# All tokens of k and v five to a partition on 116 partitions, the last one in a transfer of its own

## Chip, cores, metric

One core of one Trainium2 chip. The metric is device time in microseconds (us) of one execution. The profile is a hardware trace of one execution; its span is some 2 us shorter than the time that is measured for that run.

## The reference

Linear attention with the map elu + 1, followed by one feed-forward layer with GELU (tanh form), float32 in and out:

```python
# q, k, v: (8 batches, 8 heads, 576 tokens, 64)   w_in: (512, 2048)   w_out: (2048, 512)
phi = lambda x: np.where(x > 0, x, np.exp(x) - 1.0) + 1.0
q_p, k_p = phi(q), phi(k)
kv  = einsum('bhsd,bhse->bhde', k_p, v)
z   = sum(k_p, axis=2)
num = einsum('bhsd,bhde->bhse', q_p, kv)
den = einsum('bhsd,bhd->bhs', q_p, z)[..., None] + 1e-06
x   = (num / den).transpose(0, 2, 1, 3).reshape(4608, 512)
out = gelu(x @ w_in) @ w_out
```

For the argument one number counts: a batch has 576 tokens, which is 4.5 x 128.

## The kernel before

Of each batch, 512 tokens of q, k and v are loaded four to a partition on all 128 partitions. The other 64 (the "rest") of two batches share a tile of 128 partitions and come in small transfers. The main loads, the weights and the transposing transfers are all issued from SyncE, in program order, into one queue; 20 of the 24 transfers of rests come from GpSimd, and the stores from ScalarE.

```python
P = 128; C = 4; MAIN = P * C; REST = S - MAIN            # 512 and 64
pld = ctx.enter_context(tc.tile_pool(name="pld", bufs=6))  # loads and weights on their way in
psm = ctx.enter_context(tc.tile_pool(name="psm", bufs=2))  # transposed rests of q (qtr)

def load_main(src, b, name, eng, parts=1):
    t = pld.tile([P, H, C * D], FP32, name=name, tag="ld")
    hs = H // parts
    for i in range(parts):
        eng.dma_start(
            out=t[:, i * hs : (i + 1) * hs, :],
            in_=src[b, i * hs : (i + 1) * hs, 0:MAIN, :].rearrange(
                "h (p c) d -> p h (c d)", c=C))
    return t

def load_rest_half(src, t, m, s, eng):
    eng.dma_start(out=t[REST * s : REST * (s + 1)],
                  in_=src[2 * m + s, :, MAIN:S, :].rearrange("h p d -> p h d"))

def load_batch(b):
    for n, src in (("k", k), ("q", q), ("v", v)):
        ld[n, b] = load_main(src, b, n + "_x", nc.sync)

def kv_mm(b, i, kv_ps, at_i=None):                        # per pair of heads
    # ... cut: dst, kp, kr
    for c in range(C):
        nc.tensor.matmul(dst, lhsT=kp[:, c, P * i : P * (i + 1)],
                         rhs=vps[b % 2][:, 2 * i : 2 * i + 2, c, :], start=(c == 0), stop=False)
    nc.tensor.matmul(dst, lhsT=kr[:, 0, P * i : P * (i + 1)],   # the rests, in a matmul of their own
                     rhs=vrs[(b // 2) % 2][b % 2][:, 2 * i : 2 * i + 2, :], start=False, stop=True)

def qtr():                                                # q of a batch, by transposing transfers
    phis("q")
    qts[b] = pt.tile([P, C, NP, P], BF16, name="qt")
    for c in range(C):
        nc.sync.dma_start_transpose(out=qts[b][:, c],
                                    in_=phi["q", b][:, c].rearrange("p h d -> p (h d)"))
# ... cut: q @ kv (n_ps) waits for qt; x goes through transposes to h_ps (first GEMM), GELU, o_ps (second GEMM)

for b in range(4, B):
    at(2, b - 3, 2 if b == 4 else 0, lambda b=b: load_batch(b))   # the loads of b, ahead of qtr of b - 1
```

## Time and profile before

| | before |
|---|---|
| median of 4 runs (lowest to highest) | 296.93 us (295.47 to 297.31) |
| TensorE (PE) busy, granted clock | 97% of the span, 1.00 |
| transfers, whole queue when full | 406 GB/s |
| first n_ps matmul of batches 1, 2, 3, 4, 5, 6, 7 | 47.2, 77.6, 96.4, 121.4, 151.6, 181.8, 211.5 us |

The granted clock is the share of its full clock that TensorE was given. The page gives the busy share of every engine, then its course in 40 slices of the span (a digit is tenths), then the chain of work that ended last. Its lines are quoted in the prediction below. The starts of n_ps, read from the trace's list of matmuls, are the clock of this kernel: n_ps of a batch is the first matmul that needs the batch's transposed q. Before the change matmuls set the pace from 40 us on.

### The profile page before, as it was taken

To read this page: it belongs to the slowest core of one execution; us is meant where nothing else is said; L and a number is where in the kernel's file an instruction comes from. 1 tells how busy PE (TensorE), PEld (TensorE's weight loads), DVE (VectorE), ACT (ScalarE), POOL (GpSimd) and SP (SyncE) were. 2 spreads that over 40 slices of the span, in tenths; PEclk is the share of its full clock that TensorE was granted. 3 is DMA by queue.
4 is the path that set the end of the run, shared out by engine and by line. 5 is a ranking of instruction groups with operands and counts; after the bars stand their busy time and mean duration, and the time that the engine had idled before them with its cause. 6 is when DMAs were issued, how large, how long until landed. Compare 5 with 4: busy or idle time off the path is not lost.

```text
span 293.6 us, 4284 instructions
## 1 busy us (share of the span) xinstructions
PE 285.3 (97%) x1701; PEld 149.8 (51%) x1730; DVE 114.4 (39%) x189; ACT 159.2 (54%) x221; POOL 37.1 (13%) x56
## 2 busy tenths in 40 slices
PE   8999999999999999999999999999999999999995
PEld 6885446644565545544454445544554444444443
DVE  3660576245486684356125652543241000000002
ACT  4657963679955772567255935682560176017400
POOL 8057077400005200000000000000000000000000
PEclk9999999999999999999999999999999999999999
DMA  7999999994599969949913895304241110021032
GB/s 238 328 405 394 370 363 384 318 363 143 151 345 243 185 203 341 190 59 288 307 65 71 245 312 126 71 2 139 75 62 30 71 74 0 4 94 47 0 71 71
DMA packets 63731, 53.23 MB, mean 181 GB/s; under 512 B 31712, under 2 KB 56544, under 8 KB 63712
## 3 DMA queue, kind: packets, MB, share of 16 engines
q1 hardware_dynamic: 60288, 41.82, 50.7%
q10 hardware_dynamic: 2464, 8.52, 7.4%
q0 software_dynamic: 960, 2.62, 3.4%
q8 instruction: 13, 0.21, 0.3%
q14 instruction: 6, 0.05, 0.1%
HBM read 36.70 MB, written 9.44 MB: 157 GB/s over the span
## 4 chain that ended last, share of the span: by engine, by line
PE 84%; DMA 11%; DVE 2%; POOL 1%; issue 1%; SPq 0%; ACT 0%; DVEq 0%
PE o_ps L734 39%; PE h_ps L306 37%; DMA w_st<-in_moe_w_out_dram 8%; DMA q_x<-in_q_dram 3%; PE n_ps L258 3%; PE kv_ps L224 2%; PE o_ps L703 1%; POOL w_out_sb L153 1%; PE t_ps L281 1%; DVE kvbd L247 1%; PE kv_ps L231 1%; SPq L67 0%; ACT q_e L165 0%; PE t_ps L252 0%; DVE xt L388 0%
## 5 line engine op out<-in xcount | busy, mean ns | idle before, releaser
L734 PE MATMUL o_ps<-w_out_sb,g 128*128 128x512 bf16 x547 | 123.7, 379 | 1.3 <-POOL w_out_sb L153 0.4
L306 PE MATMUL h_ps<-xt,w_in_sb 128*128 128x512 bf16 (+2 forms) x566 | 118.9, 353 | 0.8
L691 ACT ACTIVATE g<-h_ps 128x512 bf16<-128x512 f32 x144 | 84.4, 598 | 49.9 <-PE h_ps L306 49.0
L734 PEld LDWEIGHTS <-g 128*128 128x128 bf16 x560 | 54.1, 98 | 63.5 <-issue 1.1
L306 PEld LDWEIGHTS <-w_in_sb 128*128 128x128 bf16 x644 | 58.2, 98 | 54.4 <-issue 0.5
L749 ACT COPY o_sb<-o_ps 128x512 f32<-128x512 f32 x18 | 10.5, 585 | 57.7 <-PE o_ps L734 53.1
L747 DVE COPY o_sb<-o_ps 128x512 f32<-128x512 f32 x17 | 11.7, 689 | 64.5 <-PE o_ps L734 57.2
L270 DVE TENSOR_TENSOR x<-n_ps,r 128x512 bf16<-128x512 f32 x36 | 24.9, 692 | 1.2
L247 DVE CAST kvbd<-kv_ps 64x260 bf16<-64x260 f32 (+1 forms) x16 | 6.5, 409 | 39.2 <-PE kv_ps L231 39.1
L165 ACT ACTIVATE q_e<-q_x 128x2048 bf16<-128x2048 f32 (+1 forms) x10 | 15.5, 1557 | 3.1 <-DMA q_x<-in_q_dram 3.1
L165 ACT ACTIVATE k_e<-k_x 128x2048 bf16<-128x2048 f32 (+1 forms) x9 | 15.5, 1719 | 2.8 <-DMA k_x<-in_k_dram 2.7
L268 DVE RECIPROCAL r<-n_ps 128x8 f32<-128x8 f32 x36 | 7.4, 206 | 24.0 <-PE n_ps L258 24.0
L182 DVE TENSOR_TENSOR k_p<-k_p,k_e 128x2048 bf16<-128x2048 bf16 (+1 forms) x9 | 10.7, 1193 | 13.5 <-ACT k_e L165 13.3
L333 PE MATMUL w_ps<-warm 128*128 128x252 bf16 x94 | 14.0, 315 | 1.1 <-DVE warm L124 1.1
L176 DVE TENSOR_SCALAR q_p<-q_x 128x2048 bf16<-128x2048 f32 (+1 forms) x10 | 10.7, 1068 | 8.8 <-DMA q_x<-in_q_dram 8.8
L306 PE MATMUL h_ps<-xt_rest,w_in_sb 128*128 128x512 bf16 x62 | 13.9, 379 | 0.1
L258 PEld LDWEIGHTS <-qt 128*128 128x128 bf16 x128 | 9.7, 98 | 7.9 <-issue 1.0
L208 DVE CAST vp<-v_x 128x2048 bf16<-128x2048 f32 (+1 forms) x9 | 9.4, 1045 | 9.9 <-DMA v_x<-in_v_dram 9.9
L258 PE MATMUL n_ps<-kvbd,qt 128*128 128x130 bf16 x128 | 12.7, 221 | 0.6 <-ACT kvbd L247 0.2
L224 PEld LDWEIGHTS <-k_p 128*128 128x128 bf16 x128 | 9.6, 96 | 6.1 <-DVE vp L208 0.7
L224 PE MATMUL kv_ps<-vp,k_p 128*128 128x130 bf16 x128 | 11.9, 220 | 0.4 <-DVE vp L208 0.4
L333 PEld LDWEIGHTS <-warm 128*128 128x128 bf16 x94 | 10.4, 114 | 3.2 <-DVE warm L124 1.1
(52 smaller groups left out, 141.3 us busy)
## 6 DMA issues: line engine op xcount, KB each, us to landing
out_dram<-o_sb ACTq DMA_DIRECT2D x16, 512.0 KB, 4.9
k_x<-in_k_dram SPq DMA_DIRECT2D x7, 1024.0 KB, 5.9
v_x<-in_v_dram SPq DMA_DIRECT2D x7, 1024.0 KB, 12.4
q_x<-in_q_dram SPq DMA_DIRECT2D x6, 1024.0 KB, 9.0
w_st<-in_moe_w_in_dram SPq DMA_DIRECT2D x4, 1024.0 KB, 10.1
w_st<-in_moe_w_out_dram SPq DMA_DIRECT2D x4, 1024.0 KB, 11.3
q_x<-in_q_dram SPq DMA_DIRECT2D x4, 512.0 KB, 9.9
k_x<-in_k_dram SPq DMA_DIRECT2D x2, 512.0 KB, 4.1
```

The source lines that it names most:

```text
L165: nc.scalar.activation(e[:, :, hs, :].rearrange("p c h d -> p h c d"), by_chunk(x[:, hs]), AF.Exp)
L176: nc.vector.tensor_scalar(xp[:, :, hs, :].rearrange("p c h d -> p h c d"), by_chunk(x[:, hs]), 1.0, 1.0, op0=ALU.add, op1=ALU.max,)
L182: nc.vector.tensor_tensor(xp[:, :, hs, :], xp[:, :, hs, :], e[:, :, hs, :], op=ALU.min)
L224: nc.tensor.matmul(dst, lhsT=kp[:, c, P * i : P * (i + 1)], rhs=vps[b % 2][:, 2 * i : 2 * i + 2, c, :], start=(c == 0), stop=False,)
L258: nc.tensor.matmul(n_ps[rows, i // 2, 2 * E * (i % 2) : 2 * E * (i % 2) + 2 * E], lhsT=qt_c[:, i, rows], rhs=kvbd[:, i, :], skip_group_che ...
L270: nc.vector.tensor_tensor(x, n_v[:, :, :, 0:D], r[:, :, :, None].to_broadcast([P, 2, 4, D]), op=ALU.mult,)
L306: nc.tensor.matmul(h_ps[:, tok], lhsT=w_in_sb[:, c, P * m : P * (m + 1)], rhs=xt[:, c, tok], start=(c == 0), stop=(c == KM - 1), skip_grou ...
L333: nc.tensor.matmul(w_ps[:, 0:252], lhsT=warm[:, 0:P], rhs=warm)
L691: nc.scalar.activation(gs[j][:, i, :], ps, AF.Gelu_apprx_tanh)
L734: nc.tensor.matmul(o_pss[t], lhsT=g[:, m, P * t : P * (t + 1)], rhs=w_out_sb[:, m, :], start=(m == 0), stop=(m == MM - 1),)
L747: nc.vector.tensor_copy(dst, o_ps)
L749: nc.scalar.copy(dst, o_ps)
```

## The change

The intent is to have no rest of k and v any more: 575 tokens lie five to a partition on 115 partitions, the last token's five-group (tokens 571 to 575, four of them loaded twice) on partition 115 by a transfer of its own, and only partition 115's fifth token is used. That takes away the small rest loads, their maps and casts and GpSimd's clearing of their tiles. To make room, the pools psm and px lose a buffer each. Cut to the core:

```diff
+    CK = 5
+    PK = S // CK          # 115
+    RK = PK + 1           # 116
-    psm = ... bufs=2      px = ... bufs=5
+    psm = ... bufs=1      px = ... bufs=4
+    def load_kv(src, b, name, parts=1, eng=nc.sync):
+        t = staged(name, LD).rearrange("p (h x) -> p h x", h=H)
+        eng.dma_start(
+            out=t[PK:RK],
+            in_=src[b, :, S - CK : S, :].rearrange("h (p c) d -> p h (c d)", c=CK),
+        )
+        hs = H // parts
+        for i in range(parts):
+            s = slice(i * hs, (i + 1) * hs)
+            nc.sync.dma_start(
+                out=t[0:PK, s],
+                in_=src[b, s, 0 : PK * CK, :].rearrange("h (p c) d -> p h (c d)", c=CK),
+            )
+        return t[0:RK]
     def load_batch(b):
-        for n, src in (("k", k), ("q", q), ("v", v)):
-            ld[n, b] = load_main(src, b, n + "_x", nc.sync)
+        ld["k", b] = load_kv(k, b, "k_x")
+        ld["q", b] = load_q(b, "q_x", nc.sync)      # q as before
+        ld["v", b] = load_kv(v, b, "v_x")
     # kv_mm:
-        for c in range(C):
+        for c in range(CK):
+            r = slice(0, RK if c == CK - 1 else PK)
             nc.tensor.matmul(
                 dst,
-                lhsT=kp[:, c, P * i : P * (i + 1)],
-                rhs=vps[b % 2][:, 2 * i : 2 * i + 2, c, :],
+                lhsT=kp[r, c, P * i : P * (i + 1)],
+                rhs=vps[b % 2][r, 2 * i : 2 * i + 2, c, :],
-        nc.tensor.matmul(dst, lhsT=kr[...], rhs=vrs[...], ...)
# ... cut: all loads, maps, casts and memsets of kr and vr go; q's rests stay
```

## The prediction

> **What bounds the kernel now.** I read the page first. Its second part says where the time is and where it is not: the tensor engine is busy 97% of the span at the full granted clock, and the transfers are near full only in the first third.
>
> ```profile
> span 293.6 us, 4284 instructions
> PE 285.3 (97%) x1701; PEld 149.8 (51%) x1730; DVE 114.4 (39%) x189; ACT 159.2 (54%) x221; POOL 37.1 (13%) x56
> ...
> PEclk9999999999999999999999999999999999999999
> DMA  7999999994599969949913895304241110021032
> ...
> PE 84%; DMA 11%; DVE 2%; POOL 1%; issue 1%; SPq 0%; ACT 0%; DVEq 0%
> ```
>
> The last line is the chain that ended last: 84% matmuls, 11% transfers, next to nothing else. The 11% lie wholly at the start. The chain in order of time, for the first 45 us, shows it:
>
> ```profile
> 2.34 8.66 DMA q_x<-in_q_dram
> ...
> 14.28 13.33 DMA w_st<-in_moe_w_out_dram
> 27.66 8.97 DMA w_st<-in_moe_w_out_dram
> 36.68 3.02 POOL w_out_sb L153 x2
> 39.75 1.89 PE o_ps L734 x8
> ```
>
> So up to about 40 us the kernel runs at the pace of the transfer queue, and from there at the pace of matmuls. Next, how fast the queue is when it is full. A window from 15 to 25 us, and the queue's own row:
>
> ```profile
> 15.00:25.00 10.00, 9.35 (x130) 7.73 (x129) 4.89 (x13) 5.48 (x10) 6.07 (x6) 1.00 1.05 406
> ...
> q1 hardware_dynamic: 60288, 41.82, 50.7%
> ```
>
> All 16 engines are busy (share 1.05) and move 406 GB/s, 25.4 GB/s each. The queue q1 of SyncE holds all loads of k, q, v and the weights and also all the transposing transfers. Last, the transposes, once behind loads and once on a quiet queue (the tile qt, windows 87 to 93 and 199 to 206 us):
>
> ```profile
> L465 SPq DMA_TRANSPOSE qt<-q_p x4: 1257/1262/1637, 87.4 to 91.7; - x4
> ...
> DMA to landing us min/median/max: 3.5/4.8/5.5
> ```
>
> ```profile
> L465 SPq DMA_TRANSPOSE qt<-q_p x4: 1191/1257/1264, 200.0 to 203.9; - x4
> ...
> DMA to landing us min/median/max: 2.3/2.4/2.4
> ```
>
> The reader is to see that a transpose takes 2.3 us alone and up to 5.5 us behind a load. The completion records agree: v of batch 4 lands at 92.36 us and the transpose issued at 87.35 lands at 92.89. It waited in the queue for the loads ahead of it.
>
> **What the Trainium skill says.** (1) "DMA: Bandwidth & Descriptors", section "Why a DMA increments its semaphore by 16 and not by 1": a transfer is cut along the slowest dimension of both access patterns, over the largest number k of engines, at most 16, that divides both sizes; on the SyncE and ScalarE queues these are the lowest-numbered k; 100 partitions give 10, 127 give 1. In the kernel before every plain transfer has 128 or 64 rows outermost, so k is 16 and no run yet shows another k. (2) Same page, "Queues, rings and completion order": on each engine one queue's work is consumed in the order of issue. The transposes above agree. (3) "TensorE: Matmul & The Clock Gate", Part 1: an idle window of some 3.4 us halves the clock. Not seen before (1.00 in every window), and possible after.
>
> **The change, part by part.** *Removed:* 16 rest loads of k and v (128 KB each, 4 from SyncE and 12 from GpSimd), the GpSimd memsets of vr and kr_p in the first 8 us, five kr maps and eight vr casts. *Added:* a fifth token on each partition, and a one-partition transfer per load. Vector and scalar work nets out: with 2560 columns for 2048 the k exp goes from 1.91 to about 2.33 us, and two batches add 0.84, against one 0.61 us kr exp removed; on VectorE the three k and v operations gain some 0.85 us a batch, 1.7 for two, against 0.42 + 0.42 + 2 x 0.42 = 1.7 removed. Matmuls stay five for a head pair, 160 in all. None of this is on the chain, so without the transfers I would call it 297 us.
>
> *The transfers are what moves.* The main load has 115 partitions outermost on both sides, 115 = 5 x 23, so by the skill's rule it runs on engines 0 to 4 alone. Cost of a load: with a full queue, k and q of batch 2 land 2.72 and 2.81 us after what is ahead of them; an engine's share is 64 rows of 1024 B, so 42 ns a row. Weight loads land 2.56 us apart for 32 rows of 2048 B, 80 ns a row. The line through both gives 51.6 ns for a row of 1280 B. Each of five engines gets 23 partitions x 8 heads = 184 rows: **9.5 us a load in place of 2.7** (an estimate; 124 GB/s). There are 16 such loads, and engines 0 to 4 still do their sixteenth of everything else.
>
> *The first stage.* The first half of k lands at 4.48 us with 1.35 us of transfer, so 3.1 us are fixed. Before, to the end of v of batch 3: 3.1 + 12 x 2.7 (k, q, v) + 8 x 2.56 (weights) + 2.8 (four rests on SyncE) + 2.6 (two stores) + 5.9 (rests of GpSimd) = 67.3 us; it landed at 71.7, so 4.4 us are unexplained and I keep them. After: 3.1 + 8 x 9.5 + 4 x 2.7 + 20.5 + 2.6 + 2.0 + 4.4 = 119.4 us. On the way v of batch 0 lands at about 25 us (before 14.8) and v of batch 1 at about 65 to 68 (before 43.0): the matmuls start 10 us late, and are 22 to 24 us late in the second half of batch 0. Then the transposes of batch 2's q stand in the same queue behind v of batch 3, and its first n_ps matmul, at 77.6 us before, has to wait for about 120: **+42 us**.
>
> *The later stages.* The program issues the loads of batch b+1 ahead of the q transposes of batch b, and every such transpose now waits for two loads of 9.5, one of 2.7 and two stores of 1.3 us: 24.3 in all. Batch 3: 119.4 + 2.9 (four transposes of 0.72) + 24.3 + 0.5 = 147 us for 96.4 before, +51. From there it is a loop: n_ps begins; the four x transposes and the next k load follow after 8.0 us (batch 3) or 10.7 us (batches 4, 5), as before; then 2.4 us to start, 24.3 of transfers, 0.5 to the first transpose. Batch 4: 147.1 + 8.0 + 27.2 = 182.3 for 121.4, +61. Batch 5: 182.3 + 10.7 + 27.2 = 220.2 for 151.6, +69. Batch 6: 258.1 for 181.8, +76. The period is 37.9 us where matmuls alone need 30.2. Batch 7 has no load behind it; from 181.8 us on the kernel before needs 111.8 us, mostly matmuls. Sum: 258.1 + 111.8 = 369.9 span, and the medians lie 3.5 us over the span: 373. As stores and loads share the queue better than a plain sum, and five engines may each run a little faster than sixteen do together (7% would make a load 8.9 us, and 16 x 0.6 = 10 us less), I take **368 us**.
>
> **Rivals.** (a) *The load still uses 16 engines* (the software reorders or splits it): then the small rest transfers go and nothing on the chain changes but the queue of the first 40 us, which gets four rests (2.8 us) shorter: 293 to 298 us. For it: the rule was not seen at work in this trace. Against: the partition dimension can't be split into 16 and is always outermost. (b) *Five engines, but the later loads hide:* in 175 to 235 us the DMA row reads 1 to 5 tenths, which suggests room. Then only the first stage stays, +24 to +42 us: 321 to 339. Against: the transposes stand behind the loads in one queue, and a mean over 16 engines hides five full ones. (c) *Worse:* ScalarE issues the stores and may stand behind a transfer whose completion it waits for; before, it waited 4.6 us once for a v load.
>
> ```profile
> ACT o_sb L749 <- DMA v_x<-in_v_dram: 4.6, 1, 4.6
> ```
>
> If that happens with loads of 9.5 us, GELU stands too, and the tensor engine at half clock after each idle stretch adds 1 to 2 us a batch: 385 to 400.
>
> **Range and chances.** The load time is the great lever: 1 us more or less on it is 16 us. With 8.3 to 10.5 us, and the overlaps of (b) and (c), 338 to 398. Faster by over 2% would need rival (a) and more: 0.02. Within 2%: (a), 0.05. Slower: 0.93.
>
> **What would show it.** Right: k_x and v_x take 9 us or more to land even first in the queue (before, 3.7 at the least); packets of 1280 B in q1; the window around 200 us has the DMA row at three or four tenths for long while PE idles; waits of PE or VectorE for qt; n_ps of batch 2 at about 120 us; a period near 38 us from batch 4 to 6; the last 110 us unchanged. Wrong: a whole-queue rate over 300 GB/s while k or v is loaded, or PE still at 97%; then (a) holds. PE full from 130 us on would mean (b). Long ScalarE waits for a load ahead of a store would mean (c).

## The result

The changed kernel takes **421.22 us** (420.45 to 422.62, 4 runs) against 296.93 us (295.47 to 297.31, 4 runs): 1.42 times as long, with a 95% interval of 1.414 to 1.428. A ratio here is the mean time of one kernel's runs over that of the other's of the same rounds, so not quite the ratio of the medians that are quoted. Executions over 1.5% slower than the fastest of the same kernel are left out of the means. The output is correct. Direction and mechanism are as predicted; the size is not: 421 lies above the range of 338 to 398.

The page of the changed kernel, with the lines that answer to those of before, and the row of GB/s:

```profile
span 419.2 us, 4288 instructions
PE 308.7 (74%) x1730; PEld 159.5 (38%) x1730; DVE 111.5 (27%) x171; ACT 160.5 (38%) x216; POOL 24.9 (6%) x35
...
PEclk9767986899965797599769985899679999999999
DMA  4499394593369579456833469237841431101113
GB/s 121 140 240 374 127 204 144 143 230 141 119 166 123 125 238 136 109 117 215 127 72 63 142 203 145 50 103 234 118 87 35 129 49 65 52 0 50 52 25 75
...
PE 48%; DMA 39%; SPq 9%; DVE 2%; issue 1%; ACT 0%; DVEq 0%
```

In many slices the DMA row reads 3 to 5 where it read 9 before: a third of the engines, not a quiet queue. The chain is 39% transfers and 9% SyncE's sequencer (SPq), for 11% and 0% before. The clock is below 1 in most slices of the first three quarters, 0.865 in the mean.

Two windows of the changed kernel. The columns are the window, its length, busy times by engine, then clock, mean busy share of the 16 DMA engines, GB/s:

```profile
22.00:30.00 8.00, 1.91 (x18) 1.24 (x16) 0.92 (x2) 1.28 (x2) 0.00 (x0) 0.71 1.08 239
105.00:115.00 10.00, 6.68 (x31) 2.84 (x29) 2.74 (x2) 5.41 (x7) 0.00 (x0) 1.00 0.34 119
```

In the second a k or v load is alone: 5 of 16 engines busy, 119 GB/s. The first is the surprise: all engines are busy as in the window of before that moved 406 GB/s, and they move 239.

Where the tensor engine stands for it, from the waits of the changed kernel (us in total, times, longest):

```profile
PE n_ps L248 <- DMA qt<-q_p: 67.9, 5, 16.5
...
DVE vp L210 <- DMA v_x<-in_v_dram: 42.6, 4, 21.1
```

And the chain of waits in order of time (start, duration, what), its longest transfers alone:

```profile
30.25 51.71 DMA w_st<-in_moe_w_out_dram x3
...
122.18 16.60 DMA qt<-q_p
...
151.87 19.86 DMA qt<-q_p
...
205.93 6.03 DMA qt<-q_p
...
244.18 16.95 DMA qt<-q_p
...
286.40 18.28 DMA qt<-q_p
```

Up to 82 us the weights come late because the k and v loads stand ahead of them; then, once a batch, a transposed q ends a wait. Their ends are the starts of n_ps, side by side with the prediction:

| n_ps of | before | predicted | measured | excess over predicted |
|---|---|---|---|---|
| batch 2 | 77.6 | 120 | 138.8 | 19 |
| batch 3 | 96.4 | 147.1 | 171.8 | 25 |
| batch 4 | 121.4 | 182.3 | 212.0 | 30 |
| batch 5 | 151.6 | 220.2 | 261.2 | 41 |
| batch 6 | 181.8 | 258.1 | 304.7 | 47 |
| end of the span | 293.6 | 369.9 | 419.2 | 49 |

### The profile page after: what moved, and what is told of

It reads as the page before. It is cut to its first block, busy times and chain, and to the rows that moved or that the text cites. A ratio compares the mean times of both kernels' runs of the same rounds, so it can differ in the third digit from the quotient of the medians.

```text
span 419.2 us, 4288 instructions
## 1 busy us (share of the span) xinstructions
PE 308.7 (74%) x1730; PEld 159.5 (38%) x1730; DVE 111.5 (27%) x171; ACT 160.5 (38%) x216; POOL 24.9 (6%) x35
## 4 chain that ended last, share of the span: by engine, by line
PE 48%; DMA 39%; SPq 9%; DVE 2%; issue 1%; ACT 0%; DVEq 0%
PE o_ps L702 24%; PE h_ps L296 20%; DMA qt<-q_p 19%; DMA w_st<-in_moe_w_out_dram 12%; DMA v_x<-in_v_dram 9%; SPq L87 4%; PE n_ps L248 2%; SPq L77 2%; SPq L501 2%; SPq L94 1%; PE kv_ps L221 1%; PE o_ps L671 1%; DVE kvbd L237 0%; DVE vp L210 0%; DVE k_p L187 0%
## 5 line engine op out<-in xcount | busy, mean ns | idle before, releaser
L702 PE MATMUL o_ps<-w_out_sb,g 128*128 128x512 bf16 x560 | 130.5, 391 | 11.7 <-POOL w_out_sb L161 11.7
L296 PE MATMUL h_ps<-xt,w_in_sb 128*128 128x512 bf16 (+2 forms) x580 | 127.8, 370 | 0.2
L659 ACT ACTIVATE g<-h_ps 128x512 bf16<-128x512 f32 x144 | 84.4, 598 | 112.3 <-PE h_ps L296 111.5
L248 PE MATMUL n_ps<-kvbd,qt 128*128 128x130 bf16 x128 | 15.9, 260 | 67.9 <-DMA qt<-q_p 67.9
L248 PEld LDWEIGHTS <-qt 128*128 128x128 bf16 x128 | 12.0, 118 | 78.5 <-DMA qt<-q_p 70.5
L717 ACT COPY o_sb<-o_ps 128x512 f32<-128x512 f32 x18 | 10.6, 586 | 68.9 <-PE o_ps L702 68.9
L221 PE MATMUL kv_ps<-vp,k_p 115*128 115x130 bf16 (+1 forms) x160 | 15.9, 247 | 18.8 <-DVE vp L210 13.6
L173 ACT ACTIVATE k_e<-k_x 116x2560 bf16<-116x2560 f32 (+1 forms) x9 | 18.9, 2100 | 21.4 <-DMA k_x<-in_k_dram 21.3
L221 PEld LDWEIGHTS <-k_p 115*128 115x128 bf16 (+1 forms) x160 | 13.1, 110 | 25.7 <-issue 9.1
L210 DVE CAST vp<-v_x 116x2560 bf16<-116x2560 f32 (+1 forms) x9 | 11.4, 1269 | 42.6 <-DMA v_x<-in_v_dram 42.6
L187 DVE TENSOR_SCALAR k_p<-k_x 116x2560 bf16<-116x2560 f32 (+1 forms) x9 | 12.1, 1339 | 20.3 <-DMA k_x<-in_k_dram 20.3
L193 DVE TENSOR_TENSOR k_p<-k_p,k_e 116x2560 bf16<-116x2560 bf16 (+1 forms) x9 | 12.1, 1344 | 11.2 <-ACT k_e L173 11.0
L173 ACT ACT_TABLE_LOAD x7 | 9.0, 1283 | 14.5 <-DMA k_x<-in_k_dram 14.4
```

Source lines behind the costliest of these rows:

```text
L173: nc.scalar.activation(e[:, :, hs, :].rearrange("p c h d -> p h c d"), by_chunk(x[:, hs]), AF.Exp)
L187: nc.vector.tensor_scalar(xp[:, :, hs, :].rearrange("p c h d -> p h c d"), by_chunk(x[:, hs]), 1.0, 1.0, op0=ALU.add, op1=ALU.max,)
L193: nc.vector.tensor_tensor(xp[:, :, hs, :], xp[:, :, hs, :], e[:, :, hs, :], op=ALU.min)
L221: nc.tensor.matmul(dst, lhsT=kp[r, c, P * i : P * (i + 1)], rhs=vps[b % 2][r, 2 * i : 2 * i + 2, c, :], start=(c == 0), stop=(c == CK - 1),)
L248: nc.tensor.matmul(n_ps[rows, i // 2, 2 * E * (i % 2) : 2 * E * (i % 2) + 2 * E], lhsT=qt_c[:, i, rows], rhs=kvbd[:, i, :], skip_group_che ...
L296: nc.tensor.matmul(h_ps[:, tok], lhsT=w_in_sb[:, c, P * m : P * (m + 1)], rhs=xt[:, c, tok], start=(c == 0), stop=(c == KM - 1), skip_grou ...
```

## Experiments

Sixteen kernels ran. The kernel before took 295.65 to 296.59 us (medians) on the same chips. Engine counts are read from the trace as the 4-byte completion writes of a transfer: each engine that takes part writes one.

### 1. How many engines does a transfer use? (m_rate; wrong output on purpose)

```diff
+    for i, n in enumerate((128, 112, 96, 120, 100, 115, 116, 127, 1)):
+        nc.sync.dma_start(out=t[0:n], in_=k[i % B, :, 0 : 4 * n, :].rearrange("h (p c) d -> p h (c d)", c=4))
+    for i, n in enumerate((115, 112, 3, 1)):      # rows of five tokens
+        nc.sync.dma_start(out=t5[0:n], in_=v[i, :, 0 : 5 * n, :].rearrange("h (p c) d -> p h (c d)", c=5))
```

> Wrong result on purpose: it only loads, one transfer after another into one tile, so each waits until the one ahead has landed. Rows of 1024 B, 8 heads, n partitions outermost, SyncE's queue. Theory (the number of partitions sets the number of engines, the largest divisor up to 16): with 2.4 us fixed and 42 ns a row of an engine, issue to landing is 128: 5.1 us, 112: 4.8, 96: 4.4, 120 (15 engines): 5.1, 100 (10): 5.8, 115 (5): 10.1, 116 (4): 12.1, 127 (1): 45. The completion writes (packets of 4 B) number 16 for 128 and 5 for 115. Rival (all sixteen engines always, the slowness is elsewhere): all between 4 and 6 us. Then the changed kernel's own shapes with rows of 1280 B: 115: 11.9 us or 5, 112: 5.3, 3 partitions: 2.8, 1 partition: 2.5.

Completion writes: 128, 112 and 96 partitions 16; 120 partitions 15; 100: 10; 115: **5**; 116: 4; 127: 1; 3: 3. That is the rule of the Trainium skill, "DMA: Bandwidth & Descriptors", section "Why a DMA increments its semaphore by 16 and not by 1", in every case tried. 127 partitions on one engine took 45 us at 23 GB/s. The one-partition transfer has 8 writes: with one partition the next dimension, 8 heads, counts. The rates of the other shapes are not to be trusted: stores and loads of the same kernel ran beside them, a fault of its design. In the changed kernel itself the completion writes add up to exactly 18 main loads x 5 and 16 one-partition transfers x 8 (14 in SyncE's queue, 2 in ScalarE's), with 16 for every other transfer.

### 2. The engine count alone, in both kernels (a_112, b_115, b_112)

a_112 is the changed kernel with its main load cut into 112 + 3 partitions (16 engines and 3). b_115 and b_112 are the kernel before, with k and v cut into 115 + 13 and 112 + 16.

```diff
 # a_112, in load_kv of the changed kernel
+        eng.dma_start(out=t[112:PK], in_=src[b, :, 112 * CK : PK * CK, :]...)
-                out=t[0:PK, s], in_=src[b, s, 0 : PK * CK, :]...
+                out=t[0:112, s], in_=src[b, s, 0 : 112 * CK, :]...
 # b_115 (b_112: 112), in load_main of the kernel before
+            for p0, p1 in ((0, P),) if name == "q_x" else ((115, P), (0, 115)):
+                eng.dma_start(out=t[p0:p1, ...], in_=src[b, ..., C * p0 : C * p1, :]...)
```

> The changed kernel with each main load of k and v cut into 112 partitions (16 engines) and 3 partitions; everything else as changed, with one transfer more for each load. Theory (five engines are the cause of nearly all of it): granted clock back to 1.00, no wait of the tensor engine for qt, 295 to 305 us. Rival 1 (the extra small transfers stall the issue of the large ones): still 340 us or more, as there are now more of them. Rival 2 (smaller buffers psm and px): over 310 us with waits for qtr and xt.

> The kernel before with each main load of k and v cut into 115 and 13 partitions, rows of 1024 B as before; no other part of the change is in it. Theory: a load takes 8 us on five engines in place of 2.7, and all the waits of the changed kernel come with it, in size 8/10: 370 to 405 us. Rival (wide rows, one-partition transfers or smaller buffers are needed for the loss): under 310 us.

> The control for b_115: the same kernel before with each main load cut into 112 and 16 partitions, both of which 16 divides, so the same number of transfers as b_115 and as the changed kernel. Theory: same as before within 1% (294 to 300 us). Rival (an additional transfer for each load is itself the cost): over 310 us.

| kernel | time | ratio to before |
|---|---|---|
| a_112, 3 rounds | 325.81 us (323.79 to 332.69) | 1.096 (1.091 to 1.102) |
| b_115, one look | 387.36 us | |
| b_112, 3 rounds | 311.32 us (308.27 to 314.21) | 1.049 (1.042 to 1.057) |

b_115 has all the rests, both buffers and the arithmetic of the kernel before, and still loses 92 us, with the same wait (from its waits):

```profile
PE n_ps L259 <- DMA qt<-q_p: 42.3, 5, 11.4
```

So the partition count of the load is enough to make most of the loss (92 of 124 us). Going from 5 engines to 16 gives the changed kernel 95 of its 124 us back. But both 112 kernels are slower than expected: b_112 should have been within 1% of before and is 5% off. Sixteen engines are not the whole of it. (The profiled run of a_112 was its slowest, 332.7 us; the ratio does not use it.)

### 3. Rate by shape (m_ports; wrong output on purpose)

```diff
+    for lo, hi in ((0, 128), (0, 112), (0, 64), (64, 128), (0, 96), (0, 115), (0, 120)):
+        for i, t in enumerate(ts):                # six loads in a row, rows of 1024 B, nothing beside them
+            nc.sync.dma_start(out=t[lo:hi], in_=src[i, :, 0 : 4 * (hi - lo), :]...)
```

> Wrong result on purpose: loads alone, six in a row of each shape (rows of 1024 B, n partitions), nothing else on the queues. The cut of the changed kernel's load into 112 partitions used sixteen engines and still moved only some 215 GB/s. Theory (the partitions that engines write at the same time must lie at different ports of the on-chip memory, and 128 whole partitions are the arrangement that fits): 128: 390 GB/s, 112: 210 to 250, partitions 0 to 63: about 210, 64 to 127: about 210, 96: 200 to 260, 120 (15 engines): 200 to 260, 115: 118. Rival (the rate follows from the number of engines alone): 112, 96 and both 64: 390, 120: 365, 115: 118. Last, 128 and 115 in turn: by the theory a row of the 128 load takes longer than its 46 ns.

Windows in the stretches with 128, 112, 64 and 115 partitions (columns as above; GpSimd's busy time is the only engine's):

```profile
5.00:15.00 10.00, 0.00 (x0) 1.00 1.10 352
22.00:40.00 18.00, 0.00 (x0) 1.00 1.12 260
50.00:60.00 10.00, 0.00 (x0) 1.00 1.13 206
...
105.00:130.00 25.00, 0.00 (x0) 1.00 0.34 121
```

| partitions | engines | ns of a 1024-B row (median) | GB/s |
|---|---|---|---|
| 128 | 16 | 49 | 350 |
| 112 | 16 | 68 | 260 |
| 96 | 16 | 76 | 235 |
| 120 | 15 | 86 | 205 |
| 64, lower or upper half | 16 | 89 | 204 |
| 115 | 5 | 46 | 121 to 124 |

With 128, 112 and 64 partitions the engines are equally busy, and a row takes 49 to 89 ns. The Trainium skill, "SBUF — State Buffer", section "Door 1: The DMA port swizzle (why `[64,N]` ≈ `[32,N]`)", says that the rate depends on how many of 16 ports the partitions reach and that 64 partitions in one half reach 8; the run agrees (204 against 350). By the port table there partitions 0 to 111, and 0 to 95, reach all 16, so the count of ports alone does not give the 260 and 235 measured. "DMA: Bandwidth & Descriptors", section "The descriptor swizzle", says that in a transfer of 128 partitions each engine writes one port of its own. That other shapes lack this order would explain 112, 96 and 120; the trace has no port in its records, so this stays an inference. What is shown is the rate. (The last part of m_ports, 128 and 115 in turn, had stores beside it and is not read here.)

The rate alone does not close the sums of part 2. As an estimate, a load of 112 x 8 rows of 1024 B at 260 GB/s takes 3.5 us for 2.7 before, 16 x 0.8 = 13 us of b_112's 16, and one of 1280-B rows 4.4 us, some 27 of a_112's 30. But in the trace of b_112 n_ps of batch 2 is 12.7 us late after eight of the sixteen loads, 1.6 a load and not 0.8, and the other eight add 2 us. Its weight rows take 98 ns in the mean of the first 90 us for 86 before, so the loads beside slow down too. What the additional transfers cost, and in a_112 the single buffer of part 5, these runs do not separate.

### 4. Ten engines (a_110)

The diff is that of a_112 with 110 for 112: 110 + 5 partitions, ten engines and five.

> As a_112, but cut into 110 and 5 partitions: 110 gives ten engines of 11 partitions, so one step between the five of the changed kernel (421 us) and the sixteen of a_112 (326 us), with the same number of transfers. Theory (the number of engines sets it): a load takes 88 rows of 60 to 75 ns, 5.3 to 6.6 us; 335 to 365 us. Rival (a transfer is either spread well or not at all): at either end, under 330 or over 400 us.

371.17 us, somewhat above what was expected, and between 421 (five engines) and 326 (sixteen), as a dose would have it.

### 5. The rivals inside the program: order, tails, a single buffer (a_order, a_tailpool, a_rest)

```diff
 # a_order: loads of batches 4 to 7 behind the q transposes of the batch before
-        at(2, b - 3, 2 if b == 4 else 0, lambda b=b: load_batch(b))
+        at(2, b - 3, 15 if b == 4 else 6, lambda b=b: load_batch(b))
 # a_tailpool: the one-partition transfers of batches 4 to 7 from GpSimd
-        ld["k", b] = load_kv(k, b, "k_x")
+        ld["k", b] = load_kv(k, b, "k_x", eng=nc.gpsimd if b > 3 else nc.sync)     # v alike
 # a_rest: the transpose of the third rest of q at another place
-        plan_rest(m, (2, 2 * m - 2, 9), (1, 2 * m, 14))
+        plan_rest(m, (1, 3, 15) if m == 2 else (2, 4, 9), (1, 2 * m, 14))
```

> The changed kernel with the loads of a later batch issued after the q transposes of the batch ahead, not before them (batches 4 to 7); the same transfers. Theory (from batch 3 on the loss is that the transposes stand behind five-engine loads in one queue): the waits of n_ps for qt in batches 3 to 6 go, the wait at batch 2 stays (n_ps of batch 2 at about 139 us), 350 to 370 us. Rival (five engines are simply full, whatever the order): over 400 us, with the waits at k_x and v_x.

> The changed kernel with the one-partition transfers of batches 4 to 7 issued from GpSimd, off SyncE's queue. SyncE stood 4 to 6 us in each of these at 144, 188, 239 and 280 us. Theory (SyncE stands there only because the queue ahead is full; the small transfer is not a cost): within 1% of the changed kernel, 417 to 425 us. Rival (each stand delays the main load behind it): 395 to 412 us.

> The changed kernel with the transpose of the third q rest moved behind the first use of the second one, so that it does not wait for the single qtr buffer at 212 to 223 us at the head of SyncE's queue. Theory (that wait held back the x transposes and the loads of batch 6 by some 8 us): 409 to 415 us, and the loads of batch 6 issued 10 us after n_ps of batch 4, not 19. Rival (the loads of batch 6 were early enough anyway): 418 to 423 us.

a_order **417.73**, a_tailpool 420.42, a_rest 417.16 us (changed kernel 421.22).

a_order was my theory, and it fell as far as it was tried. If the loss were that transposes stand behind loads in one queue, turning them round should have given 50 us or more. It gave 4. The waits of a_order show where it went:

```profile
DVE vp L210 <- DMA v_x<-in_v_dram: 51.7, 5, 20.7
...
PE n_ps L248 <- DMA qtr<-qr_p: 33.4, 2, 19.7
```

The wait for qt turned into waits for v, k and the rest transposes (qtr). n_ps of batch 3 did begin 10.6 us earlier (161.1 for 171.8 us), but then TensorE stood 19.7 us for a qtr that was issued behind the loads, and n_ps of batch 4 was only 3.6 us earlier. So a_order turned round one kind of transpose only; an order with all of them ahead of the loads was not tried. The packet records of the changed kernel say how much there was to gain: from 4 to 173 us five rows or more are under way nearly all the time (for 1.3 us near 140 they are not), from 173 to 305 us only 75% of the time. Up to 173 us the five engines are full, whatever stands first; for the rest it is not shown.

a_tailpool came out within 1% as expected: the extra small transfers are no cost. a_rest went after one stall in SyncE's timeline in the changed kernel (start, duration, what):

```profile
205.93 6.19 SPq L443 DMA_TRANSPOSE qt<-q_p  x4
212.22 12.09 SPq L491 DMA_TRANSPOSE qtr<-qr_p  x2
224.41 2.52 SPq L477 DMA_TRANSPOSE xt<-x  x2
```

With psm cut to one buffer the second qtr waits at the head of the queue until n_ps has used the first, at 223 us, and the loads of batch 6 go out 19.0 us after n_ps of batch 4 began, where 10.7 were predicted. In a_rest they go out after 14.6 us, and the kernel gains 4 us, less than the 6 to 12 expected. This stall is real and small. The smaller px was not tried alone; the trace has one wait that may be its, 3.6 us of VectorE at 227 us until a transfer of x had ended.

### 6. Why do rows get slower when all engines run? (m_mix, m_store, m_halves, m_halves2; wrong output on purpose)

```diff
 # m_mix: weight loads (16 engines, 2048-B rows) alone, five-engine loads (115 partitions, 1280-B rows) alone, in turn
+    for fns in ((weight, weight), (five, five), (five, weight), (five, weight)):
+        for i in range(6):
+            fns[i % 2](i)
 # m_store: five-engine loads alone, stores of 1 MB alone, then in turn
+    for i in range(6):
+        five(2 + i % 4)
+        store(3 + i)
 # m_halves2: five-engine loads of 25 partitions and 16-engine loads of partitions 64 to 127, alone and in groups of 2 + 2
+    for at in (0, 64):                            # where the five-engine loads go
+        for i in range(8):
+            five(2 * i, at); five(2 * i + 1, at); weight(2 * i + 4); weight(2 * i + 5)
```

> Wrong result on purpose: six weight loads (128 partitions, rows of 2048 B), six loads of the changed kernel's shape (115 partitions, rows of 1280 B), then twelve in turn, nothing else beside. Theory (the two shapes get in each other's way, so that a five-engine load costs more than its own 10 us when others run on the eleven other engines): weights 400 GB/s, 115 alone 118 GB/s (10.0 us a load), a pair in turn 15 us or more, with rows of 1280 B at 100 ns while both run. Rival (the sum that the prediction used): a pair takes 10.0 + 2.6 = 12.6 us and the rows stay at 58 ns.

> Wrong on purpose; only transfers: four five-engine loads (115 partitions, rows of 1280 B) after two weight loads, three sixteen-engine stores alone, then six pairs of a five-engine load and a store of 1 MB. Beside weight loads the rows of the five took 105 to 111 ns for 55 alone, also when the others wrote the other half of the partitions. If what they share is the writing into the on-chip memory, stores, which only read it, leave the rows of the five at 55 to 65 ns and a pair takes the sum of the two alone, about 12.3 us. If it is the engines' own path or the main memory, rows go to 90 ns or more beside stores too, and a pair takes about 14 us, as with weights.

> Wrong on purpose; only transfers. Five-engine loads of 55 partitions (55 = 5 x 11, rows of 1280 B, 440 rows) and sixteen-engine loads of the 64 upper partitions (rows of 2048 B, 256 rows), in five stretches: six five-engine loads into partitions 0 to 54 alone, six into 64 to 118 alone, six sixteen-engine loads into 64 to 127 alone, then eight pairs with the five-engine load in the lower half, then eight pairs with it in the upper half, where the sixteen-engine loads go. In the run with pairs before, a 1280-byte row took 55 ns with the five alone and 105 to 111 ns while the eleven other engines moved weights. If what they share is the way into the partitions (the ports of the on-chip memory, which are other ones for the two halves by the Trainium skill), the rows of the five in the lower half stay at 55 to 70 ns beside the others, and those in the upper half take 100 ns or more; a pair then takes some 5 to 5.5 us in the lower and 7 us or more in the upper half. If it is the engines, their queue or the memory that the data comes from, both stretches of pairs look alike, with rows near 105 ns beside the others in both. Alone, both halves should show 55 ns a row and 4.8 us a load.

> Wrong on purpose; only transfers. The run before was mis-designed: 55 partitions have 11 as a divisor too, so its loads ran on eleven engines and not on five (440 rows of 94 ns in 3.46 us). Here the five-engine loads have 25 partitions (25 = 5 x 5, 200 rows of 1280 B): ten into partitions 0 to 24 alone, ten into 64 to 88 alone, six sixteen-engine loads into 64 to 127 alone (2048-byte rows), then eight times two five-engine and two sixteen-engine loads with the five in the lower half, then eight times with them in the upper half, where the sixteen-engine loads go. Alone: 55 ns a row and 2.2 us a load in both halves. If the ways into the partitions are what the two kinds share, rows of the five beside the others stay at 55 to 70 ns in the lower half and take 90 ns or more in the upper half, and a group of four loads is shorter in the lower half by 1 us or more. If they share engines, queue or the memory the data comes from, both stretches look alike.

m_mix measures the term that the prediction's sum rests on. In its windows (weights alone, five alone, and both at once):

```profile
8.00:18.00 10.00, 0.00 (x0) 1.00 1.05 387
22.00:80.00 58.00, 0.00 (x0) 1.00 0.33 124
95.50:98.50 3.00, 0.00 (x0) 1.00 1.07 229
```

By the packet records the loads follow each other every 2.7 us (weights), every **9.55 us** (five engines; predicted 9.5), and a pair every **13.95 us**, where the two add up to 12.25. While the eleven other engines move weights (the third window), a row of the five takes 107 ns in the mean for 55 alone, and a weight row 145 for 89. The 13.95 lies between the theory (15 or more) and the rival (12.6), so the theory was right in kind and too large.

m_store has the same pairs with stores for weights. Its windows, five alone and with a store beside them:

```profile
54.00:57.00 3.00, 0.00 (x0) 1.00 0.33 124
58.00:60.00 2.00, 0.00 (x0) 1.00 0.98 390
```

Beside stores a row of the five still takes 55.0 ns, a pair takes 12.0 us, its plain sum (9.53 + 2.46), and the whole queue moves 390 GB/s. So sharing engines and a queue is not enough to slow the rows: in these runs loads disturb the five and stores do not. The stores went in packets of 8192 B, though, the weights in 2048 B; that difference no run separates.

m_halves failed by its design: 55 partitions have the divisor 11, and its "five-engine" loads ran on eleven engines (440 rows of 94 ns in 3.46 us). m_halves2 mended that. (By the section "Door 1" cited in part 3, the two halves reach different ports.) Alone, rows take 55 ns in either half. In groups, with the five in the half that the other loads do not write, a group takes 9.1 us, its plain sum (2 x 2.08 + 2 x 2.46 = 9.1); in the same half 10.3 us. That part went as the port theory expected. Its other part failed: in separate halves the rows still slow down while more than five rows of the others are under way (112 ns in the median, against 133 in the same half, and 55 alone). The half that is written takes part, which fits the ports but does not show them; whether the rest is the on-chip memory's side or the main memory's is not settled.

### 7. The same idea on all 128 partitions (a_128, a_128r, a_128z)

a_128 keeps "no rests", with four tokens on each of 128 partitions and tokens 448 to 575 one to a partition in a fifth place, of which the fifth matmul uses the upper 64. a_128r adds the edit of a_rest. a_128z makes v's fifth place (and its ones) zero on partitions 0 to 63, so that this matmul has all 128 rows.

```diff
 # a_128
-    RK = PK + 1
+    RK = P
+                out=t[:, s, 0 : C * D], in_=src[b, s, 0:MAIN, :].rearrange("h (p c) d -> p h (c d)", c=C)
+        eng.dma_start(out=t[:, :, C * D : CK * D], in_=src[b, :, S - P : S, :].rearrange("h p d -> p h d"))
-            r = slice(0, RK if c == CK - 1 else PK)
+            r = slice(P - REST if c == CK - 1 else 0, P)
 # a_128z, from a_128r
+            r = slice(0, P)
+        nc.gpsimd.memset(vps[i][0 : P - REST, :, C, :], 0.0)
+        fn(out=vps[b % 2][:, s, 0:C, 0:D], in_=v4[:, :, 0:C])
+        fn(out=vps[b % 2][P - REST : P, s, C, 0:D], in_=v4[P - REST : P, :, C])
```

> The changed kernel with its intent kept (five tokens to a partition in one tile, no rest maps or casts of k and v, the same smaller buffers), but loaded in shapes of 128 partitions: four tokens to a partition as before, and tokens 448 to 575 one to a partition in the fifth place, of which partitions 64 to 127 are used. Theory (the shapes of the transfers are the whole loss): 294 to 302 us, clock 1.00. Rival (smaller buffers, or the wider vector and scalar work, cost as well): 306 to 320 us with waits for qtr or x.

> a_128 together with the edit of a_rest (the third q rest's transpose does not wait for the single qtr buffer). In a_128 that wait stood at 131 to 137 us at the head of SyncE's queue, the loads of batch 6 went out at 145 us (before: 132), and the tensor engine then waited 9 us for qt at 154 to 163 us. Theory: this accounts for 7 to 10 of the 16 us by which a_128 is slower than before: 302 to 307 us, and no wait for qt over 3 us; the rest is the first 40 us, where the added rows of 256 B (a fifth place for 128 partitions) are carried by a full queue. Rival: the loss in a_128 is all in the first stage, 310 us or more.

> The version on 128 partitions with the moved transpose, now with the fifth place zero in v (and in its column of ones) on partitions 0 to 63, so that the fifth matmul of a head pair takes all 128 rows and not the upper 64. In the version before, five kv matmuls with a 64-row one among them took 0.49 us from the first to the next h_ps, against 0.30 us in the kernel before and in the changed kernel: 0.2 us each, 0.8 us a batch, 6 us in all; its n_ps starts slip by just that, 0.85 us a batch. If that is the cause, the period from batch 5 to 6 falls from 31.05 to about 30.2 us and the time from 307 to about 301 us. If the slip comes from the longer vector operations (five places for four), the period stays at 31 and the time at 306 to 309.

| kernel, 3 rounds | time | ratio to before |
|---|---|---|
| a_128 | 312.95 us (310.43 to 314.68) | 1.059 (1.054 to 1.064) |
| a_128r | 307.33 us (305.68 to 309.18) | 1.041 (1.036 to 1.045) |
| a_128z | 303.45 us (302.63 to 304.81) | 1.025 (1.020 to 1.031) |

a_128 missed its 294 to 302. The stall of the single qtr buffer is 5.6 us of that (a_128r; 7 to 10 were expected). In a_128r the starts of n_ps slip evenly against those of before, by 0.8 us a batch (batch 4 at 128.9 for 121.4, batch 7 at 221.5 for 211.5). The timeline of TensorE shows it, here a_128r and then the kernel before:

```profile
216.59 0.56 PE L221 MATMUL kv_ps<-vp,k_p 128*128 128x130 bf16 x5
217.07 1.04 PE L296 MATMUL h_ps<-xt,w_in_sb 128*128 128x512 bf16 x4
217.95 0.56 PE L221 MATMUL kv_ps<-vp,k_p 128*128 128x130 bf16 x5
```

```profile
207.20 0.40 PE L224 MATMUL kv_ps<-vp,k_p 128*128 128x130 bf16 x4
207.43 0.22 PE L231 MATMUL kv_ps<-vr,kr_p 128*128 128x130 bf16 x1
207.49 1.02 PE L306 MATMUL h_ps<-xt,w_in_sb 128*128 128x512 bf16 x4
208.35 0.40 PE L224 MATMUL kv_ps<-vp,k_p 128*128 128x130 bf16 x4
```

From one pair of heads to the next it is 1.36 us in a_128r (216.59 to 217.95) and 1.15 before (207.20 to 208.35): a 64-row matmul among 128-row ones costs 0.2 us, four times a batch. (The line shows the first form; the trace lists 32 of the 160 as 64 rows.) In a_128z:

```profile
215.69 0.45 PE L221 MATMUL kv_ps<-vp,k_p 128*128 128x130 bf16 x5
215.98 1.03 PE L296 MATMUL h_ps<-xt,w_in_sb 128*128 128x512 bf16 x4
216.84 0.45 PE L221 MATMUL kv_ps<-vp,k_p 128*128 128x130 bf16 x5
```

The step is 1.15 us again. The time fell by 4 us, not by the 6 expected, and the trace has a wait for a transpose that a_128r does not have (n_ps for qt, twice, 2.2 us in all), which may have taken part of it back. a_128z is the best version of the idea and still 2.5% slower than before: it is 5 us behind at n_ps of batch 1 already, where w_out lands at 39.3 us for 36.6. No version beat the kernel before.

## Why the prediction was wrong in size

**What bounds the kernel, and what the change leaves alone: right.** Matmul counts stay, and the k exp takes 2.33 us as worked out. VectorE's busy time falls from 114.4 to 111.5 us and ScalarE's rises from 159.2 to 160.5. b_115 shows that none of this is needed for the loss.

**Five engines: right.** Five completion writes per load, share 0.34 with a load alone. Rival (a), sixteen engines anyway, is out.

**"9.5 us a load in place of 2.7": right for a load alone; the sum that is built on it is the step that failed.** It measures 9.55 us alone. But the sum "3.1 + 8 x 9.5 + 4 x 2.7 + 20.5 + ..." adds five-engine loads and sixteen-engine loads as if neither disturbed the other, and the last paragraph even took 5 us off because "stores and loads share the queue better than a plain sum, and five engines may each run a little faster". Of that, nothing came true: stores add up to the plain sum and no better (m_store: 12.0 us for a pair), five engines alone take the 9.5 us, and for loads the opposite holds: a pair takes 13.95 us for 12.25, **1.7 us per five-engine load**. In the changed kernel the 1280-B rows take 67 ns in the mean, the same 67 ns as in m_mix's pairs. An estimate from that: eight loads in the first stage make 13.6 of the 19 us of excess at batch 2, and two loads a batch make 3.4 us in each of four later stages. From the issue of k to the first transposed q it is indeed 30.6, 30.2 and 30.9 us in batches 4 to 6, for 27.2 predicted: 3.4 more in the mean. That the two agree so closely may be chance in part, as only one q load a batch lies between.

**"n_ps begins; ... the next k load follow after 8.0 us (batch 3) or 10.7 us (batches 4, 5), as before": wrong in one place.** It measures 9.6, 19.0 and 12.7. The 19.0 is the single qtr buffer, which I passed over in the diff (8 us in the table; a_rest gave 4 of them back). The other two are 1.6 and 2.0 us long, in stages where the clock falls.

**The sum.** Of 47 us of excess at batch 6, by these readings: some 27 contention among loads, 8 the qtr stall, 4 the slower stretches; the remaining 8 (5 in the first stage, 3 at batch 3) are not assigned. The first stage was slow from its start: v of batch 0 landed at 31.5 us where the prediction had about 25. The end adds 3 (114.5 us for "111.8 us unchanged"), and the 5 that I had taken off come on top, less 1.5 because the time lies 2.0 us over the span and not 3.5. 368 + 47 + 3 + 5 - 1.5 = 421.

**Rivals.** (b), later loads hide, is out: the excess grows to batch 6. Its counterpart, that they fail to hide *because of the order*, was implied by my "the transposes stand behind the loads"; a_order gained 4 us by turning round the transposes of qt, and no run turned round all of them. (c) is half right. The clock fell (0.865), as the Trainium skill, "TensorE: Matmul & The Clock Gate", Part 1, has it for idle stretches: TensorE stood ten times for 4.9 to 16.5 us, each time the granted clock went to 0.5 and stayed there for 3.4 to 17 us, and n_ps matmuls took 260 ns in the mean for 221. ScalarE stood too, 36 us for k (21.3 + 14.4) and 8.3 for v, but the wait that I named, a store's copy behind a v load, is not among its waits any more; what its standing cost, no run separates.

**The range** allowed 1 us more per load on the ground that sixteen such us decide. It is 1.7, plus a buffer.

## What to carry to other kernels

Before cutting a load to an odd number of partitions, look at the largest divisor up to 16 of its outermost size: 115 has 5, 116 has 4, 127 has 1. Then do not stop at "sixteen engines": of the seven shapes timed here only 128 partitions ran at full rate, and a load on few engines slowed full loads beside it and was slowed by them, so that the two took longer than the sum of both alone. An idea that saves instructions on engines with time to spare should be tried on 128 full partitions, with full-row matmuls, before it is given up, and every buffer that it gives away should be traced to the queue whose head it can stop.

## What the Trainium skill lacked or had wrong

- "DMA: Bandwidth & Descriptors", "Rules for kernel authors", asks for an outermost size that is a multiple of 16, ideally the 128 partitions, to use all 16 engines. That is right for the count (112 and 96 partitions: 16 completion writes), but the page does not say how much rate the other multiples lose: 260 GB/s with 112 partitions, 235 with 96, 204 with 64, 350 with 128. The section "The descriptor swizzle" covers 128 partitions alone.
- Same page, section "Why a DMA increments its semaphore by 16 and not by 1": the rule for the number of engines held in every shape tried (128, 120, 112, 100, 96, 116, 115, 127). What a transfer on few engines costs has to be worked out from the "Specifications", some 27 GiB/s (29 GB/s) an engine, and measured less: five engines move 119 to 124 GB/s, one 23.
- No page that I found has a number for how loads on few engines and loads on sixteen slow each other ("SBUF — State Buffer", "SBUF: two separate sides", only names the DMA ports as a place where engines can contend): 1280-B rows 107 ns for 55, 13.95 us for a pair whose parts take 12.25, while beside stores they stay at 55 ns.
- "SBUF — State Buffer", "Door 1", agrees on one half (204 against 350 GB/s). Its count of ports does not give the rates of 112 and 96 partitions (260 and 235), and separate halves did not free five-engine loads from slowing beside the others (112 ns a row in the median for 55).
- No page that I found has the cost of a 64-row matmul on the upper rows between 128-row ones; here 0.2 us each (1.36 us a step for 1.15). "TensorEngine Tiling (Array Packing)", "Key Properties", says that changing the tiling mode drains the engine; whether that is what happens here, no run shows.
